# Delta-rule recurrence and MLP on one core: first chunk's inverse in 64x64 tiles, and a new hand-written order of all queues

## The chip, the cores and the metric

The kernel runs on one core of a Trainium2 chip. The core has a matrix engine (TensorE, PE in the profile; its weight loads are PEld), VectorE (DVE), ScalarE (ACT), GpSimd (POOL) and SyncE (SP), which here only issues DMAs. Each engine works off its own list of instructions in order. Matrix results go to PSUM, eight banks of 2 KB a partition, which GpSimd can't read. The metric is the time of one execution in microseconds on the device; lower is better.

## The reference

There are 4 x 8 = 32 heads with 768 steps and a head dimension of 48. Each head keeps a 48x48 state that is read by the query and corrected by the delta rule; the rows of all heads of a step, 384 numbers, then go through an MLP with 2048 hidden units.

```python
k_n = k / (np.linalg.norm(k, axis=-1, keepdims=True) + 1e-06)
for t in range(S):
    y[:, :, t] = np.einsum('bhd,bhde->bhe', q[:, :, t], state)
    v_old = np.einsum('bhde,bhd->bhe', state, kt)
    state = state + bt[:, :, :, None] * np.einsum('bhd,bhe->bhde', kt, vt - v_old)
...
x = y.transpose(0, 2, 1, 3).reshape(B * S, H * D)
out = gelu_tanh(x @ w_in) @ w_out
```

The line for the output stands before the update, so a step does not see its own key.

## The kernel before, in words

The 768 steps are cut into 12 chunks of C = 64. Within a chunk the recurrence is solved with matrices: with A the strictly triangular 64x64 matrix of scaled key products of a head, the corrected values are (I + A)^-1 (v - K S), and what a chunk adds to the state and to the output are plain products. The partitions hold two batches at once (64 steps each), so a **unit** u is 16 of the 32 heads and a chunk has two units, 2c and 2c+1; there are 24.

`prep(u)` (line 461) makes a unit ready. kn, kb and qb are the normed keys (L476), the keys times beta (L478) and the queries, in bf16. T transposes them on TensorE (L486) and kT copies them out; from unit 10 on a DMA does that. G2 and G (L508, L500) are the products of keys; ln and wp (L512, L516) copy them under a mask into tiles whose other triangle was written beforehand ("backgrounds", `tri` for ln and `triw` for wp, in `preset`, line 371). Then comes the inverse, five iterations in the loop from L521 on. Two 64x64 blocks stand on the diagonal of a 128x128 tile bd, so one matmul of 128 rows does both batches. X1 (L525, GpSimd) puts the first estimate there, one half at a time; A (L535) multiplies bd with wp or ln, rt (L542, VectorE) adds twice the identity, B multiplies bd with that, and the result goes back into bd in two half copies (bde, by ScalarE or VectorE), or once into the compact tile xi and from there by GpSimd (bdc, L529). The last result is xi. In the last two iterations only the columns from 16 or 32 on are made (A16, A32).

`chain(c)` (line 554) is what must go chunk by chunk: K and R (keys times state, less v), U (xi times that, L601), S (the state's update, L610), O and Q (output, L624, L579), X (its transposition, L645). For the first chunk K, Q and R are replaced by a copy of v. `mlp(gi)` (line 652) takes the 256 rows of a chunk: 16 groups `up` of three matmuls (L666), four GELUs, and two rows of four `down` groups of four matmuls (L678), whose results go out through SP.

**What sets the order.** Nothing is dynamic. `ORDER` holds a list for each engine, written out as text, and `BANKS` the PSUM bank of each TensorE operation that takes one. `Flow.schedule` gives each operation its place and `Flow.emit` puts a semaphore wait ahead of what needs one. An operation that may run on several engines names them, and the lists decide. A label is the operation's name and a running number. **Fills** (`warm_up`, line 392) are matmuls of 128x512 on zeros that no one reads; they stand in TensorE's list where the clock is to be kept up. 97 of them stand there, 87 ahead of U.0.

**Loads.** `load` reads q, k and v of a chunk in three rotating buffers (SP's list; the first chunk's k in halves, also by ScalarE). `weights` (line 427) has four transfers of 768 KB, which GpSimd issues; its list stands still meanwhile. They are declared as readers of the second and third chunk's k and q, so that they wait until those have come.

Of the kernel before, what the change touches and what calls it, by code (L numbers as in the profile page):

```python
# [5 lines left out]
F32 = mybir.dt.float32  # L6
BF16 = mybir.dt.bfloat16
# [11 lines left out]
        fill.0 fill.1 fill.2 fill.3 fill.4 fill.5 fill.6 fill.7 fill.8 fill.9 fill.10 fill.11 fill.12 fill.13 fill.14 fill.15 fill.16  # L19
        fill.17 fill.18 fill.19 fill.20 fill.21 fill.22 fill.23 fill.24 fill.25 fill.26 fill.27 betaT.0 fill.28 fill.29 fill.30  # L20
        fill.31 fill.32 fill.33 fill.34 fill.35 fill.36 fill.37 fill.38 T.0 fill.39 fill.40 T.1 G2.0 G.0 fill.41 fill.42 fill.43
        fill.44 fill.45 G2.1 G.1 fill.46 fill.47 fill.48 fill.49 fill.50 A.0 fill.51 fill.52 fill.53 fill.54 B.0 A.3 fill.55 fill.56
        fill.57 fill.58 B.5 A.1 fill.59 fill.60 fill.61 fill.62 fill.63 B.1 A.4 fill.64 fill.65 fill.66 fill.67 B.6 A.2 fill.68
        fill.69 fill.70 A.5 fill.71 fill.72 B.2 fill.73 B.7 T.2 fill.74 fill.75 fill.76 fill.77 A16.1 A16.0 fill.78 G2.2 fill.79 B.8
        B.3 fill.80 T.3 A32.1 fill.81 fill.82 A32.0 fill.83 B.9 B.4 G.2 fill.84 G2.3 fill.85 fill.86 U.0 fill.87 fill.88 A.6 G.3 S.0
        fill.89 B.10 O.0 K.0 fill.90 fill.91 fill.92 A.7 A.9 T.4 B.11 X.0 B.15 fill.93 fill.94 fill.95 fill.96 A.8 G.4 up.4 A.10 up.5
        B.12 up.6 B.16 up.8 A16.2 up.9 up.7 up.10 A.11 up.11 B.13 G2.4 up.0 B.17 up.1 up.12 up.2 up.13 up.3 up.14 A16.3 A32.2 A.12
        up.15 T.5 B.18 down.4 B.20 down.5 G2.5 G.5 A32.3 B.14 down.6 B.19 A.13 down.7 Q.0 U.1 B.21 down.0 A.15 O.1 A.14 B.25 down.1
        S.1 X.1 down.2 B.22 A.16 K.1 down.3 B.26 A16.4 up.20 up.28 up.21 up.29 B.23 A.17 T.6 up.30 B.27 up.31 up.22 G2.6 up.23 A16.5
        A32.4 G.6 up.24 B.28 up.16 up.25 up.17 A.18 up.18 A32.5 B.24 up.19 B.30 up.26 T.7 B.29 T.8 up.27 A.19 down.12 G2.7 G.7 G2.8  # L30
        B.31 down.13 G.8 U.2 down.14 A.20 down.15 A.21 A.24 B.32 T.9 B.35 down.8 A16.6 B.40 down.9 G2.9 Q.1 O.2 G.9 B.33 down.10 A.22
        X.2 A.25 down.11 B.36 A32.6 up.36 A.27 up.37 B.34 B.41 up.38 A.23 B.45 up.32 up.39 up.33 B.37 up.34 up.40 up.35 up.41 A.28
        up.42 A16.7 A.26 up.43 up.44 B.46 down.20 B.38 B.42 up.45 S.2 up.46 A32.7 down.21 A16.8 up.47 A.29 B.39 down.16 B.43 K.2
        down.22 B.47 down.23 Q.2 U.3 down.17 A32.8 A16.9 down.18 O.3 S.3 down.19 X.3 B.48 G2.10 G.10 B.44 up.52 up.60 up.53 K.3 G2.11
        up.61 up.54 up.62 A32.9 up.63 A.30 up.56 up.55 up.57 B.50 up.58 G.11 B.49 up.59 up.48 A.31 up.49 U.4 G2.13 A.33 B.51 up.50
        up.51 G.13 Q.3 O.4 G2.12 B.55 A.39 X.4 A.32 G.12 down.28 B.65 up.64 B.52 A.34 up.65 up.68 up.66 A.40 up.67 A.36 up.69 B.56
        A16.10 up.70 B.66 B.60 up.71 up.76 B.53 up.77 A.35 up.78 A.37 up.79 down.24 A.41 B.61 B.57 up.72 A32.10 down.25 A16.11 B.67
        A.38 down.26 up.73 B.58 S.4 B.62 up.74 A16.13 down.27 up.75 A16.12 down.29 K.4 B.68 B.54 A32.11 down.32 B.63 B.59 down.33
        down.36 U.5 Q.4 down.34 A32.12 down.35 O.5 A32.13 down.37 G2.14 S.5 G.14 down.38 B.64 B.69 down.39 K.5 G2.15 G.15 down.30 U.6
        Q.5 A.42 down.31 up.80 A.45 up.81 B.70 up.82 O.6 A.43 up.83 up.92 G2.17 G.17 up.93 up.84 up.94 B.71 B.75 up.95 up.85 G2.16  # L40
        up.86 A.46 up.87 G.16 up.88 B.76 up.89 A.51 up.90 A.44 A.48 up.91 B.85 A.47 B.72 down.40 B.80 up.104 down.41 B.77 up.105 A.52
        A.49 down.42 up.106 B.81 up.107 A16.14 down.43 up.100 B.86 up.101 A16.15 up.96 B.73 up.97 up.102 B.78 up.103 up.98 A.50 up.99
        A32.14 A.53 up.108 B.82 up.109 A32.15 S.6 up.110 B.79 B.87 up.111 down.44 K.6 B.74 A16.16 down.45 A16.17 U.7 B.83 B.88 down.46
        down.48 Q.6 S.7 down.49 O.7 G2.18 G.18 down.47 down.50 A32.17 A32.16 down.51 G2.19 K.7 A.54 B.84 down.52 B.89 B.90 down.53
        G.19 down.54 A.55 U.8 G2.20 G.20 down.55 A.57 up.120 B.91 up.121 B.95 up.122 G2.21 up.123 A.60 G.21 A.58 A.56 B.100 up.124
# [87 lines left out]
class Flow:  # L133
# [34 lines left out]
    def schedule(self, order, banks):  # L168
        seen, label = {}, {}
        for o in self.ops:  # L170
            kind = o.name.lstrip("01")
            label[f"{kind}.{seen.setdefault(kind, 0)}"] = o
            seen[kind] += 1
# [102 lines left out]
def bass_deltanet__then__act_gelu_tanh_kernel(  # L276
# [13 lines left out]
    NU = 2 * NC  # L290
    DIRECT = lambda u: (2, 3, 4, 5) if u < 8 else (2, 4)
    GROUPS = [[c] for c in range(NC)]
    TURN, TURNX = 10, 5

    F = Flow()
    A = F.add

    with nc.allow_non_contiguous_dma("strided loads"), nc.allow_low_precision("bf16 pipeline"):
# [39 lines left out]
        def hf(a, n=C):  # L338
            return slice(64 * a, 64 * a + n)
# [406 lines left out]
```

## Time and profile before

| what | value |
|---|---|
| median of 3 runs | 283.89 us (283.83 to 288.8) |
| the profiled execution | 283.22 us |
| its span, first to last instruction | 281.5 us |
| mean granted TensorE clock | 0.981 |
| DMA traffic | 29.71 MB, mean 106 GB/s |

The profile is of one execution. Its page gives the busy time of each engine, then the span in 40 slices of 7 us with a digit for each (tenths busy; PEclk is the clock that was granted to TensorE, in tenths), then the DMA queues, the chain of work that ended last, and the costliest groups of instructions. In a group or a timeline the row reads: line, engine, operation, tiles out<-in, shape, count, then busy time and idle time with the engine that ended it. "issue" means that the engine waited for nothing that the profile shows. Queue q0 carries the transfers that GpSimd asks for, q1 those of SP and ScalarE, and q8 and q14 are named "instruction". The windows view cuts the span in stretches and gives for each the length, then busy time and count of each engine, the granted clock, the mean share of the DMA engines' time (over 1 where packets queue) and the rate. The span outside the program (1.7 us of the execution's time) is the same for every kernel.

### The profile page before, as it was taken

Reading aid. Unit: us, or ns where it says so; the run is one execution under the profiler, and the core shown is the slowest. Engines: PE = TensorE matmul, PEld = TensorE weight load, DVE = VectorE, ACT = ScalarE, POOL = GpSimd, SP = SyncE. Lnnn points to the kernel's source line nnn. Section 1 sums busy time; section 2 is a strip of 40 time slices with the busy share of each in tenths; the row PEclk is TensorE's granted clock in tenths of the full one; section 3 lists DMA queues with packets and bytes.
Section 4 is the critical chain, followed back from the end, with each engine's and each line's share of the span. In section 5 each row is a group of like instructions: output and inputs, shape, how many; then the busy total and the mean of one; then the engine's idle time right before and its main releaser. Section 6 shows DMA issues by size and latency. Waiting matters only on the chain.

```text
span 281.5 us, 12649 instructions
## 1 busy us (share of the span) xinstructions
PE 264.2 (94%) x5726; PEld 200.4 (71%) x5737; DVE 198.9 (71%) x307; ACT 173.5 (62%) x261; POOL 144.9 (51%) x224
## 2 busy tenths in 40 slices
PE   8999957999999999979999899999999989999994
PEld 3555645877887887758876678976788777778762
DVE  6488963899899977867776699866898576752000
ACT  7678544788776976475872476645686546523541
POOL 3376653179895899767653872845546132110000
PEclk9999995999999999997999999999999999999999
DMA  5999999942919519996546980498819330043004
GB/s 106 164 153 180 189 191 149 153 75 41 133 36 175 105 33 174 143 152 135 94 88 121 160 123 2 87 171 144 156 30 148 68 72 2 2 56 73 21 14 98
DMA packets 109237, 29.71 MB, mean 106 GB/s; under 512 B 103296, under 2 KB 108416, under 8 KB 109184
## 3 DMA queue, kind: packets, MB, share of 16 engines
q1 hardware_dynamic: 105696, 25.57, 58.2%
q0 software_dynamic: 2880, 3.15, 7.2%
q8 instruction: 45, 0.74, 1.2%
q10 hardware_dynamic: 608, 0.20, 0.3%
q14 instruction: 8, 0.07, 0.1%
HBM read 20.64 MB, written 4.72 MB: 90 GB/s over the span
## 4 chain that ended last, share of the span: by engine, by line
PE 82%; DVE 6%; issue 4%; POOL 4%; ACT 2%; DVEq 0%; POOLq 0%
PE ps L666 22%; PE ps L678 21%; PE ps L535 19%; PE ps L394 6%; PE ps L579 2%; PE ps L486 2%; PE ps L624 2%; PE ps L508 2%; POOL nrm L455 2%; PE ps L601 2%; PE ps L500 2%; PE ps L610 1%; DVE wp L516 1%; DVE ln L512 1%; POOL tok L478 1%
## 5 line engine op out<-in xcount | busy, mean ns | idle before, releaser
L666 PE MATMUL ps<-xT,W 128*128 128x256 bf16 x576 | 83.0, 273 | 0.0
L678 PE MATMUL ps<-W,gT 128*128 128x384 bf16 x384 | 76.5, 328 | 0.7 <-issue 0.7
L342 ACT ACTIVATE bd<-ps 64x512 bf16<-64x512 f32 x93 | 54.2, 589 | 25.7 <-PE ps L535 24.0
L671 ACT ACTIVATE gT<-ps 128x1024 bf16<-128x1024 f32 x48 | 48.5, 1022 | 23.9 <-PE ps L666 23.6
L542 DVE TENSOR_TENSOR rt<-ps,two 128x512 bf16<-128x512 f32 x72 | 48.2, 687 | 11.7 <-PE ps L535 10.8
L666 PEld LDWEIGHTS ps<-xT,W 128*128 128x128 bf16 x576 | 48.7, 98 | 7.3 <-ACT gT L671 0.3
L525 POOL TENSOR_SCALAR_AFFINE_SELECT bd<-ln 64x512 bf16<-64x512 bf16 x48 | 31.4, 657 | 32.9 <-DVE ln L512 29.5
L529 POOL COPY bd<-xi 64x256 f32<-64x256 f32 x64 | 25.3, 397 | 39.7 <-ACT xi L342 24.9
L678 PEld LDWEIGHTS ps<-W,gT 128*128 128x128 bf16 x384 | 32.6, 98 | 17.2 <-issue 1.4
L342 ACT ACTIVATE xi<-ps 128x512 bf16<-128x512 f32 x42 | 24.4, 595 | 16.0 <-PE ps L535 15.8
L516 DVE CAST_PREDICATED wp<-mup,ps 128x1024 bf16<-128x1024 uint16 x24 | 29.0, 1214 | 2.3 <-PE ps L500 2.3
L542 DVE TENSOR_TENSOR rl<-ps,two 128x384 bf16<-128x384 f32 (+1 forms) x48 | 22.8, 485 | 9.2 <-PE ps L535 8.8
L535 PE MATMUL ps<-rt,bd 128*128 128x64 bf16 x576 | 28.7, 195 | 0.3 <-issue 0.2
L455 POOL TENSOR_TENSOR nrm<-nrm,half 128x16 f32<-128x16 f32 x9 | 26.4, 2928 | 4.2 <-DVE nrm L452 4.0
L535 PEld LDWEIGHTS ps<-rt,bd 128*128 128x128 bf16 x576 | 24.3, 99 | 5.5 <-DVE rt L542 2.4
L535 PE MATMUL ps<-wp,bd 128*128 128x64 bf16 (+1 forms) x576 | 27.3, 189 | 0.5 <-DVE rt L542 0.2
L478 POOL TENSOR_TENSOR tok<-tok,bsb 128x384 bf16<-128x384 bf16 x24 | 20.2, 850 | 14.6 <-DVE tok L476 7.7
L535 PEld LDWEIGHTS ps<-wp,bd 128*128 128x128 bf16 x576 | 23.6, 98 | 5.5 <-issue 1.5
L342 DVE CAST bd<-ps 64x512 bf16<-64x512 f32 x35 | 24.0, 686 | 4.9 <-PE ps L535 4.4
L394 PE MATMUL ps<-wz 128*128 128x512 bf16 x86 | 24.5, 410 | 2.2 <-DVE wz L348 1.3
L476 POOL TENSOR_TENSOR tok<-kraw,nrm 128x384 bf16<-128x384 f32 x22 | 18.1, 829 | 6.8 <-DVE nrm L459 6.7
L342 ACT ACTIVATE ob<-ps 128x384 f32<-128x384 f32 x20 | 9.7, 490 | 18.9 <-PE ps L678 18.6
(84 smaller groups left out, 341.9 us busy)
## 6 DMA issues: line engine op xcount, KB each, us to landing
qraw<-in_q_dram SPq DMA_DIRECT2D x24, 192.0 KB, 5.5
vraw<-in_v_dram SPq DMA_DIRECT2D x24, 192.0 KB, 5.5
out_dram<-ob SPq DMA_DIRECT2D x47, 96.0 KB, 3.1
kraw<-in_k_dram SPq DMA_DIRECT2D x22, 192.0 KB, 4.8
W<-in_moe_w_in_dram POOLq DMA_DIRECT2D x2, 768.0 KB, 8.6
W<-in_moe_w_out_dram POOLq DMA_DIRECT2D x2, 768.0 KB, 10.3
kraw<-in_k_dram SPq DMA_DIRECT2D x3, 96.0 KB, 3.4
kT<-tok SPq DMA_TRANSPOSE x14, 4.6
```

The costliest lines, as they stand in the source:

```text
L342: return e.activation(out, in_, ACT.Copy) if e is nc.scalar else e.tensor_copy(out, in_)
L394: return e.matmul(P(f"fill{i}")[:, :], wz[:, 0:128], wz[:, 0:512])
L455: e.tensor_tensor(nr[:, 1, hx], nr[:, 0, hx], half[:, hx], ALU.pow),
L478: A(POOL, z + "kb", lambda e, P: e.tensor_tensor(kb, kn, bcol, ALU.mult), reads=[n("tok0"), *BS], writes=[n("tok1")], pos=u)
L516: A("dve", z + "wp", lambda e, P: e.copy_predicated(wp[s][:, :, :], mup[:, :].bitcast(U16).unsqueeze(1).to_broadcast([128, H, 2 * C]), P(p ...
L525: A("pool", z + "X1", lambda e, P, src=src, dst=dst: e.affine_select(out=dst, in_=src, compare_op=ALU.not_equal, fill=1.0, base=0, pattern ...
L529: A("pool", z + "bdc", lambda e, P, src=src, dst=dst: e.tensor_copy(dst.bitcast(F32), src.bitcast(F32)), reads=[n("xi")], writes=[w(f"bd{a ...
L535: ins = e.matmul(P(name)[:, C * h + lo:C * h + C], bd[m][:, h, :], rhs[:, h, lo:C])
L542: A("dve", z + f"rt{lo or str()}", lambda e, P, i=i, lo=lo, r_=r_: e.tensor_tensor(r_[:, :, lo:C], P(ps(f"A{i}")).rearrange("p (h t) -> p ...
L666: ins = e.matmul(P(ph)[:, w * f:w * f + w].rearrange("p (x t) -> p x t", x=2), W1[:, j, 128 * (i + f):128 * (i + f) + 128], x_[:, :, j, :] ...
L671: A("act", z + "gelu", lambda e, P, i=i, ph=ph: e.activation(g_[:, i:i + nf, 0:w], P(ph).rearrange("p (f t) -> p f t", f=nf), ACT.Gelu_app ...
L678: ins = e.matmul(P(po)[:, 0:DM], g_[:, f, 128 * b:128 * b + 128], W2[:, f, :], start=(f == 0), stop=(f == FC - 1))
```

## The change

Six things are changed at once.

1. For units 0 and 1 (`TILED` = 2) the inverse runs in the compact tile xi. X1t is one addition of ln and twice the identity on GpSimd or VectorE, without bd. Each product At or Bt is 16 matmuls of 64x64, two tiles of the array, in place of 8 of 128x128. The result is copied once into xi. All 64 output rows are made as before, and the last two At start at columns 16 and 32.
2. For these two units the masked copy wp is cut in two (wph), so that the inverse waits for the first half alone, and O for the second ("wq").
3. GpSimd may write the backgrounds; the new lists let it write triw for three of the six wp tiles and tri for one of the four ln tiles. For units 2 to 5 VectorE may scale the keys (the lists leave that on GpSimd) and ScalarE may copy the queries (it does so for units 2 and 3). kT of any unit may be copied by ScalarE (unit 9 is).
4. The weight transfers no longer wait for other loads. In GpSimd's list two of them now stand side by side behind unit 3's kb, the third behind X1 of unit 2, the last behind kn of unit 5.
5. Labels are name.position/number instead of name.number.
6. All five lists and the banks are new. There are 111 fills. 87 stand ahead of the first U, 99 ahead of the first up, and the others singly or in threes up to chunk 8.

```diff
-    TURN, TURNX = 10, 5
+    TURN, TURNX, TILED = 10, 5, 2
...
-                    A(("act", "dve"), z + ("tri" if w == C else "triw"), lambda e, P, t=t, w=w: copy(
-                        e, t[s][:, :, :], tmpl[:, 0:w].unsqueeze(1).to_broadcast([128, H, w])), reads=["tmpl", "tmplz"], writes=[f"{n}{s}"], pos=2 * s - 9)
+                    A(("act", "dve", "pool"), z + ("tri" if w == C else "triw"), lambda e, P, t=t, w=w: copy(
+                        e, t[s][:, :, :], tmpl[:, 0:w].unsqueeze(1).to_broadcast([128, H, w])) if e is not nc.gpsimd else
+                      e.tensor_copy(t[s][:, :, :].bitcast(F32), tmpl[:, 0:w].bitcast(F32).unsqueeze(1).to_broadcast([128, H, w // 2])),
+                      reads=["tmpl", "tmplz"], writes=[f"{n}{s}"] + ([f"wq{s}"] if w > C else []), pos=2 * s - 9)
...
-                  reads=[f"{n}raw1{x}" for n in "kq" for x in range(2)], writes=[f"W1{i}"], dma=f"w1{i}", pos=-3 + 0.1 * i)
+                  writes=[f"W1{i}"], dma=f"w1{i}", pos=-3 + 0.1 * i)
...
-                  reads=[f"{n}raw2{x}" for n in "kq" for x in range(2)], writes=[f"W2{i}"], dma=f"w2{i}", pos=-2 + 0.1 * i)
+                  writes=[f"W2{i}"], dma=f"w2{i}", pos=-2 + 0.1 * i)
...
+            if u < TILED:
+                A(("dve", "pool"), z + "X1t", lambda e, P: e.tensor_tensor(
+                    xi[s][:, :, :], ln[m][:, :, :], two[:, :].unsqueeze(1).to_broadcast([128, H, C]), ALU.add), reads=[w("ln"), "two"],
+                  writes=[n("xi")], pos=u)
+                for i in range(1, 6):
+                    con, conn = (wp[s][:, :, 0:C], n("wp")) if i % 2 else (ln[m], w("ln"))
+
+                    def product(e, P, name, rhs, lo):
+                        for h in range(H):
+                            for a in range(2):
+                                ins = e.matmul(P(name)[hf(a), C * h + lo:C * h + C], xi[s][hf(a), h, :], rhs[hf(a), h, lo:C])
+                        return ins
...
+                    A(EV, z + "xi", lambda e, P, i=i: copy(e, xi[s][:, :, :].rearrange("p h t -> p (h t)"), P(ps(f"B{i}"))),
+                      frees=[ps(f"B{i}")], writes=[n("xi")], pos=u)
+                return
```

The start of the new lists of TensorE (from the first T to the first up) and of GpSimd:

```diff
+        fill/31 fill/32 fill/33 fill/34 fill/35 fill/36 fill/37 fill/38 fill/39 fill/40 fill/41 T.0/0 fill/42 fill/43 fill/44 fill/45
+        fill/46 fill/47 fill/48 T.1/0 G2.0/0 G.0/0 fill/49 fill/50 fill/51 fill/52 fill/53 G2.1/0 fill/54 fill/55 At.0/0 G.1/0 fill/56
+        fill/57 fill/58 Bt.0/0 fill/59 At.1/0 fill/60 At.0/1 fill/61 fill/62 Bt.1/0 fill/63 fill/64 fill/65 fill/66 At.1/1 Bt.0/1
+        fill/67 fill/68 fill/69 Bt.1/1 At.0/2 fill/70 fill/71 T.2/0 Bt.0/2 At.1/2 fill/72 fill/73 At.0/3 Bt.1/2 fill/74 T.3/0 At.1/3
+        Bt.0/3 G2.2/0 fill/75 fill/76 Bt.1/3 fill/77 fill/78 fill/79 fill/80 fill/81 At.1/4 At.0/4 G.2/0 fill/82 Bt.1/4 Bt.0/4 fill/83
+        fill/84 fill/85 fill/86 A.2/0 U.0.5/0 G2.3/0 fill/87 fill/88 B.2/0 fill/89 O.0.7/0 G.3/0 S.0.5/0 fill/90 fill/91 fill/92
+        fill/93 fill/94 A.2/1 X.0.8/0 fill/95 fill/96 fill/97 A.3/0 B.2/1 K.2.5/0 fill/98 up.3.25/0 B.3/0 up.3.25/1 A.2/2 T.4/0
...
+        tmplz.-11/0 masks.-12/2 bdz.5/0 two.-12/0 two.-12/1 ident.-29/0 triw.-9/0 masks.-12/0 triw.-7/0 ident2.-29/0 half.-28/0
+        bdz.4/0 kb.0/0 bdz.2/0 mup.-12/0 kb.1/0 mup.-12/1 masks.-12/1 mlo.-12/0 mlo.-12/1 X1t.0/0 X1t.1/0 kn.2/0 kb.2/0 kn.3/0 kb.3/0
+        tri.-3/0 w1.-3/0 w2.-1.9/0 kn.4/0 X1.2/1 triw.-1/0 X1.2/0 w1.-2.9/0 pow.6/0 X1.3/1 X1.3/0 eps.6/0 qb.5.01/0 kb.4/0 qb.4.01/0
+        kn.5/0 w2.-2/0 sq.8/0 kn.7/0 kn.6/0 X1.4/0 X1.4/1 bdz.3/0 kb.5/0 X1.5/1 X1.5/0 pow.8/0 qb.7.01/0 eps.8/0 kb.6/0 kn.9/0 kn.8/0
```

A label such as T.0/0 is the transposition of unit 0; in the text it is written T.0, and chain operations by their chunk (U.0 for U.0.5/0).

235 lines of the change are left out of this document (135 added, 100 removed), and 18 rows, old and new, of the table BANKS.

## The prediction

> **What bounds the kernel now.** I read the page first: the busy times, the slices, the shares of the chain.
>
> ```profile
> PE 264.2 (94%) x5726; PEld 200.4 (71%) x5737; DVE 198.9 (71%) x307; ACT 173.5 (62%) x261; POOL 144.9 (51%) x224
> ...
> PEclk9999995999999999997999999999999999999999
> DMA  5999999942919519996546980498819330043004
> ...
> PE 82%; DVE 6%; issue 4%; POOL 4%; ACT 2%; DVEq 0%; POOLq 0%
> ```
>
> TensorE is the bound from end to end, but two things on these lines are not arithmetic: 4% of the chain is "issue", time in which TensorE waited for nothing the profile shows, and the slices hold one dip of the clock to half and one to 0.7. The chain of waits, cut to 34 to 52 us, shows the largest piece, and the prices that I use for single operations.
>
> ```profile
> 34.47 0.61 PE ps L601 x32
> ...
> 36.20 0.56 issue
> ...
> 37.01 0.32 PE ps L610 x32
> ...
> 40.18 3.58 issue
> ...
> 50.15 0.23 PE ps L535 x8
> 50.38 0.33 PE ps L666 x3
> ```
>
> TensorE stops for 3.58 us in the middle of one transpose group, whose data were ready. To see why, I cut the windows view at the two stops above and at later ones, and at equal counts of instructions between them.
>
> ```profile
> core 0: us, PE busy (x) PEld busy (x) DVE busy (x) ACT busy (x) POOL busy (x), PEclk, DMA share, GB/s
> 14.66:22.62 7.96, 7.65 (x141) 4.31 (x140) 6.58 (x11) 6.55 (x10) 4.52 (x7) 1.00 1.33 150
> 22.62:30.86 8.24, 7.77 (x131) 5.00 (x131) 7.46 (x13) 6.09 (x12) 5.45 (x8) 1.00 1.24 186
> 30.86:36.76 5.90, 4.87 (x129) 3.42 (x129) 5.10 (x9) 3.20 (x7) 5.17 (x8) 1.00 1.32 191
> 36.76:43.76 7.00, 3.10 (x125) 2.47 (x127) 3.47 (x4) 2.69 (x4) 3.61 (x6) 0.88 1.32 192
> 43.76:52.96 9.20, 8.98 (x124) 7.28 (x125) 5.91 (x9) 5.62 (x9) 1.73 (x3) 0.72 0.92 145
> 59.65:63.30 3.65, 3.65 (x139) 2.81 (x140) 3.52 (x7) 3.00 (x5) 2.04 (x5) 1.00 0.11 20
> 121.17:126.57 5.40, 3.30 (x139) 2.66 (x133) 3.38 (x5) 3.91 (x6) 3.23 (x5) 1.00 1.10 146
> 223.08:226.54 3.46, 2.70 (x149) 2.10 (x141) 2.52 (x4) 0.81 (x1) 1.94 (x4) 1.00 0.12 26
> ```
>
> From one stop to the next, 36.76 to 43.76, stand 127 weight loads and as many matmuls (two matmul records are missing): 256 instructions with two that wait for semaphores. The other windows are cut at the same count (those full of small matmuls also count the ones that reach over an edge), and the stops fall on such edges. The DMA view says what TensorE waits for; the first line is from 35.2 to 40.6 us, the second from 40.6 to 42.2.
>
> ```profile
> q0 software_dynamic: 963, 0.73, 99.2%
> ```
>
> ```profile
> q8 instruction: 1, 0.02, 5.9%
> ```
>
> The queue of instructions moved nothing up to 40.6, while q0, which carries only the MLP weights that GpSimd asked for, took nearly the whole of the engines; then one block of 16 KB came and TensorE went on at 43.76. So TensorE runs on blocks of 256 instructions, the next but one is asked for when a block ends, and a block can't pass faster than its successor arrives. The rows give that time where TensorE was starved: 5.90 and 7.00 us with weights under way, 5.40 with loads alone (121.17), 3.46 in quiet (DMA share 0.12). At 59.65 a block passed in 3.65 us without a stop. The Trainium skill, "Runtime: NRT & Kernel Launch", section "Instruction fetch mechanics", has the blocks of 256 but says that crossing a boundary is "mostly hidden"; the 3.58 us row speaks against it here, and what its rule would make of the time is the second rival.
>
> **The change part by part.**
>
> Compact products. Each of 20 products (two units, five A and five B) becomes 16 matmuls of 64x64 in place of 8 of 128x128. An old one takes 0.23 us (the x8 row). For a new one the nearest row is U, the same shape of diagonal tiles with 48 columns: 0.61 us for 32, so 0.31 for 16, and 0.41 if it grows with 64 columns. I take 0.36, both ends kept: 20 x 0.13 = 2.6 us more TensorE time (1.6 to 3.6), and 320 instructions more. The Trainium skill, "TensorEngine Tiling (Array Packing)", section "Key Properties", says that different tiles can execute in parallel; by it 16 halves would take what 8 wholes took, and the 2.6 would be 0. The U row, whose tiles are in the same two quadrants, does not show that gain whole.
>
> What it gives back is evacuation. An iteration of the first units ran like this:
>
> ```profile
> 16.68 1.25 PE L394 MATMUL ps<-wz 128*128 128x512 bf16 x5
> 17.77 0.40 PE L535 MATMUL ps<-wp,bd 128*128 128x64 bf16 x8
> ```
>
> ```profile
> 19.57 1.21 ACT L342 ACTIVATE bd<-ps 64x512 bf16<-64x512 f32 x2 [0.87 <-PE ps L535]
> ```
>
> ```profile
> L342 ACT ACTIVATE xi<-ps 128x512 bf16<-128x512 f32 x42 | 24.4, 595 | 16.0 <-PE ps L535 15.8
> ...
> L478 POOL TENSOR_TENSOR tok<-tok,bsb 128x384 bf16<-128x384 bf16 x24 | 20.2, 850 | 14.6 <-DVE tok L476 7.7
> ```
>
> Two half copies (1.21 us) become one whole (0.595): 0.6 us saved an iteration, less 2 x 0.13 for the slower products, so 0.35 x 5 = 1.7 us on the chain. X1 on GpSimd becomes an addition of 512 columns, 850 x 512/384 = 1.1 us against two selects. Splitting wp in two costs VectorE some 0.3 us. But the fills decide when the chain may go: the new order puts 42 fills and the beta transposes ahead of T.0 and 7 more ahead of T.1. At 0.217 us a fill (five from 16.68 to 17.77),
>
> ```profile
> 1.25 7.81 PE L394 MATMUL ps<-wz 128*128 128x512 bf16 x28 [1.25 <-DVE wz L348]
> 8.99 0.93 PE L406 MATMUL ps<-identf,braw 32*128 32x32 f32 x12
> ...
> 14.54 0.32 PE L508 MATMUL ps<-kT 48*64 48x64 bf16 x16
> ```
>
> the 28 ahead of betaT become 26, which starts at 8.6; 16 more fills put T.0 at 12.9, 7 more T.1 at 15.1, and G2.0 comes at 15.8 to 16.0 against 14.54. The chain starts 1.4 us later and gains 1.7: U.0 stays at about 34.5. ScalarE issues two more loads ahead of its table load, and the first half of k goes first on SP; both are covered by the fills that hold T.0 until 12.9, and would cost about one issue (0.8 us) without them.
>
> GpSimd writes two wp backgrounds before it scales keys, and one more and one of ln behind; it waited then and has room (51% busy). The keys of units 2 to 5 stay on GpSimd, so that freedom is not used. Cost 0, covered by those waits; uncovered it is 0.75 us a background.
>
> Fills. Both orders have 87 ahead of the first U; behind it 10 become 24. That is 14 x 0.217 = 3.0 us of TensorE time, free only where TensorE would have waited.
>
> Weights. Four transfers of 768 KB were asked for at these times:
>
> ```profile
> 18.89 1.01 POOL L432 DMA_DIRECT2D W<-in_moe_w_in_dram  x1
> 23.76 0.83 POOL L476 TENSOR_TENSOR tok<-kraw,nrm 128x384 bf16<-128x384 f32 x1 [3.86 <-DVE nrm L459]
> ...
> 26.24 0.82 POOL L432 DMA_DIRECT2D W<-in_moe_w_in_dram  x1
> ...
> 31.85 0.94 POOL L436 DMA_DIRECT2D W<-in_moe_w_out_dram  x1
> ...
> 38.10 0.94 POOL L436 DMA_DIRECT2D W<-in_moe_w_out_dram  x1
> ```
>
> The dropped reads do not bring them forward: in GpSimd's new order they stand behind kn.2 (which waits for the second chunk's norm, in the old order at 23.76), kb.2, kn.3, kb.3 and a background, so the first two go at 28 and 29, next to each other, the third behind X1.2 near 34, the fourth behind kn.5 near 41. Behind each issue, 1 us, stand X1.2 and kn.4, which have that slack. By the page's list of DMA issues the slower pair lands like this,
>
> ```profile
> W<-in_moe_w_out_dram POOLq DMA_DIRECT2D x2, 768.0 KB, 10.3
> ```
>
> which is in time for the first up and down. What it does cost is that weights are under way from 28 to 52, when the new order's blocks are shortest.
>
> The sum. I counted matmuls in the new PE order, two instructions each and one more in a hundred for semaphores, the first edge at the same count as before, and priced them by the rows (up 0.33, A and B 0.23, K, Q and S 0.32, U and O up to 0.6, and from the next two the down group; the second is chunk 1's U in the timeline of TensorE).
>
> ```profile
> 58.10 0.65 PE ps L678 x4
> ```
>
> ```profile
> 62.62 0.67 PE L601 MATMUL ps<-rs,xi 64*64 64x48 bf16 x32
> ```
>
> The edges fall in G2.0 (16.0 us), At.0/1, At.1/2, behind fill 79, at U.0, X.0, G.4, T.5 and at the end of chunk 1's U. The blocks between them last 4.8, 5.4, 4.7, 4.1, 4.0, 4.8, 7.3 and 4.8 us. The old first blocks lasted 7.96 and 8.24 and hid their fetches. With 5.1 us for the first (engine waits), 5.4 for the second, 6.45 (mean of 5.90 and 7.00) for each of the next four, which can't hide it, and 7.3 and 4.8: 16.0 + 5.1 + 5.4 + 25.8 + 7.3 + 4.8 = 64.4. In the old trace that U ended at 63.2 (62.62 and 0.6). So the start is 1.2 us later. By the same prices TensorE has 197.7 us of work behind that point in the old order and 200.3 in the new: 2.6 more. Together +3.8 us. The order of the rest is new throughout, and no row prices that: from below it is the loss of every later stop (the first rival), from above as many again; I take 0, since the counts of later blocks with under 3.6 us of work are alike (seven now, eight before). The profiled execution took 283.22 us (span 281.5); the median of the runs stands 0.67 above it. 283.2 + 3.8 + 0.7 = 287.7, say 287.5.
>
> **The rivals.** Faster: fetches do not starve the start. Then U.1 ends at its price, 55.8, plus the waits of the old start (U.0 came at 34.5 with 31.7 us of work ahead of it, so 2.7), at 58.5, or 4.7 us before the old one; less the 2.6, with the 7 fills behind U.1 in waits (1.5) and one later stop and the half-clock window behind it gone,
>
> ```profile
> 126.58 0.32 PE L508 MATMUL ps<-kT 48*64 48x64 bf16 x15 [1.84 <-issue]
> ```
>
> ```profile
> 45.40:48.80 3.40, 3.18 (x36) 2.19 (x38) 1.98 (x4) 3.15 (x5) 0.09 (x1) 0.50 0.83 140
> 127.40:130.80 3.40, 3.40 (x46) 2.47 (x43) 2.66 (x4) 1.86 (x3) 2.93 (x4) 0.50 0.42 83
> ```
>
> 1.84 and half of 3.4, it comes to -4.7 + 2.6 - 1.5 - 3.5 = -7.1: 276.8 us. For it: the new blocks are evener, none under 4 us in the first 50. Against it: 4 us is still below 5.9. The rule of the Trainium skill's "Runtime: NRT & Kernel Launch" on fetches, named above, would end here.
>
> Slower: the two weight transfers asked for side by side hold a fetch longer than one did. If that adds 1.5 us to the measured 7.00 in two of the four blocks, it is 2 x (8.5 - 6.45) = 4.1 on top of the forecast: 291.8 us. It decides over 2% once the four blocks average 6.93 us, and 7.00 is a measured row. A stop of 3 us also halves the clock, as the row from 45.40 shows; that is in the old time as well, so it isn't added.
>
> No change: the waits absorb the products and the fills, and the weights' fetches stop TensorE as long as now: 284.
>
> **How the numbers follow.** The forecast (287.5; its own range is 284 to 290, by the ends 5.90 and 7.00 in four blocks, 2.2 each way, and of the products, 1.0) gets 0.33, the starved start 0.34, the free start 0.25, no change 0.08. Two per cent, about what a measurement of this kernel can tell from no change, is 278.2 and 289.6. Faster: 0.22 of the free start's 0.25. Slower: 0.34 and 0.02 of the forecast's. The rest, 0.42, is within. The range 277 to 293 leaves out some 0.12 of the free start below and 0.08 above.
>
> **What would show it.** Right: the "issue" pieces between 25 and 50 us sum to over 5 us and lie on edges of 256 instructions, the first up comes at 46 us or later, U.0 at 34 or later. A compact product of 0.31 to 0.41 us confirms the 2.6; 0.23 does not. It is wrong if the clock stays at 1.0 through 50 us and the first up comes at 42, or if a block there passes in under 4.5 us with weights under way.

## The result, and the profile after

The changed kernel takes 280.98 us (279.01 to 283.71, eight runs), the kernel before beside it 284.29 (283.74 to 288.8). The ratio is 0.9871, with a 95% interval of 0.9829 to 0.9914: 1.3% faster, clear of no change but under two per cent, where 287.5 us, 1.3% slower, was forecast. The ratios, and the medians from the next section on, are of those executions that lie within 1.5% of the fastest of their kernel; ranges are of all. The profiled execution took 279.01 us, its span is 277.2, the mean granted clock 0.998.

The page of the changed kernel, the same lines as of before:

```profile
PE 263.3 (95%) x5895; PEld 200.0 (72%) x5911; DVE 197.6 (71%) x306; ACT 168.3 (61%) x252; POOL 147.2 (53%) x226
...
PEclk9999999999999999999999999999999999999999
DMA  7996999990494679973489880659658121224004
...
PE 91%; DVE 5%; issue 2%; ACT 0%; DVEq 0%
```

"issue" fell from 4% of the chain to 2%, and both dips of the clock are gone. TensorE is busy for as long as before, though it now runs at full clock throughout: it has more to do. The chain of waits in the stretch that the prediction is about:

```profile
36.15 0.61 PE ps L665 x32
36.76 0.04 PE ps L545
36.80 0.67 issue
37.47 0.32 PE ps L545 x15
...
41.63 0.43 PE ps L431 x2
42.06 1.67 issue
43.73 0.38 PE ps L431
...
45.17 0.49 PE ps L730 x3
```

U.0 (36.15) comes 1.7 us later than before, the first up (45.17) 3.9 us earlier. The stops are 0.67 and 1.67 us instead of one of 3.58; the second stands between two fills, which lie at 41.63 and 43.73. The windows view, cut at the edges of 256 instructions:

```profile
core 0: us, PE busy (x) PEld busy (x) DVE busy (x) ACT busy (x) POOL busy (x), PEclk, DMA share, GB/s
16.77:22.08 5.31, 5.00 (x133) 2.81 (x136) 4.91 (x8) 3.23 (x6) 2.32 (x2) 1.00 1.32 142
22.08:27.66 5.58, 5.26 (x136) 3.45 (x134) 4.92 (x11) 3.40 (x7) 3.38 (x5) 1.00 0.57 103
27.66:32.35 4.69, 4.37 (x139) 3.21 (x135) 4.43 (x11) 3.58 (x9) 2.80 (x4) 1.00 0.89 138
32.35:37.47 5.12, 4.20 (x129) 2.91 (x129) 4.51 (x7) 4.92 (x8) 3.85 (x6) 1.00 1.16 190
37.47:43.73 6.26, 4.28 (x126) 3.02 (x128) 4.22 (x6) 2.36 (x4) 5.82 (x8) 1.00 1.21 203
43.73:48.32 4.59, 4.36 (x123) 4.02 (x126) 3.48 (x5) 2.64 (x5) 4.21 (x5) 1.00 0.87 129
48.32:56.10 7.78, 7.67 (x146) 6.23 (x140) 7.34 (x12) 6.01 (x10) 3.09 (x4) 1.00 1.08 174
56.10:61.10 5.00, 5.00 (x130) 3.72 (x129) 4.22 (x6) 3.62 (x7) 1.62 (x3) 1.00 1.23 155
```

The blocks that were to be held at 6.45 us each are the third to the sixth. They lasted 4.69, 5.12, 6.26 and 4.59. U.1 ends at 61.1, before at 63.2, forecast 64.4.

For the whole span I summed the pieces of over 0.1 us in which TensorE was idle at an edge of 256 ("stops" from here on; a wait that ends within eight instructions of an edge counts): 8.7 us before, 3.7 after, so 5.0 less. The half clock inside the run (42.1 to 48.9 and 127.4 to 130.8 before, none after) is the other part. TensorE was busy for 8.3 of these 10.2 us, 3.18 and 3.40 of them in the two rows at half clock that the prediction shows; taking half of that as lost (an estimate) gives 4.2. That makes 9.2 us; the span fell by 4.3. Some 5 us were given back as more work and longer chains; the first experiment shows them again.

### The profile page after: what moved, and what is told of

Read it like the earlier page. It is cut to its first block, busy times and chain, and to the rows that moved or that the text cites. A ratio compares the mean times of both kernels' runs of the same rounds, so it can differ in the third digit from the quotient of the medians.

```text
span 277.2 us, 12977 instructions
## 1 busy us (share of the span) xinstructions
PE 263.3 (95%) x5895; PEld 200.0 (72%) x5911; DVE 197.6 (71%) x306; ACT 168.3 (61%) x252; POOL 147.2 (53%) x226
## 4 chain that ended last, share of the span: by engine, by line
PE 91%; DVE 5%; issue 2%; ACT 0%; DVEq 0%
PE ps L742 23%; PE ps L730 23%; PE ps L599 19%; PE ps L431 9%; PE ps L643 2%; PE ps L688 2%; PE ps L665 2%; PE ps L537 2%; PE ps L523 2%; PE ps L570 2%; PE ps L545 2%; DVE wp L555 1%; PE ps L674 1%; DVE rt L606 1%; DVE kT L377 1%
## 5 line engine op out<-in xcount | busy, mean ns | idle before, releaser
L735 ACT ACTIVATE gT<-ps 128x1024 bf16<-128x1024 f32 x48 | 48.7, 1021 | 25.8 <-PE ps L730 25.7
L377 ACT ACTIVATE bd<-ps 64x512 bf16<-64x512 f32 x83 | 48.8, 589 | 14.4 <-PE ps L599 13.2
L606 DVE TENSOR_TENSOR rt<-ps,two 128x512 bf16<-128x512 f32 x66 | 44.1, 684 | 14.3 <-PE ps L599 13.8
L589 POOL TENSOR_SCALAR_AFFINE_SELECT bd<-ln 64x512 bf16<-64x512 bf16 x44 | 28.8, 656 | 28.2 <-DVE ln L549 25.1
L377 ACT ACTIVATE xi<-ps 128x512 bf16<-128x512 f32 x46 | 27.2, 595 | 24.1 <-PE ps L599 18.7
L431 PE MATMUL ps<-wz 128*128 128x512 bf16 x95 | 27.5, 411 | 4.4 <-issue 2.9
L555 DVE CAST_PREDICATED wp<-mup,ps 128x1024 bf16<-128x1024 uint16 (+1 forms) x26 | 29.4, 1135 | 2.2 <-PE ps L537 2.0
L599 PE MATMUL ps<-rt,bd 128*128 128x64 bf16 x528 | 25.8, 193 | 0.6 <-DVE wp L555 0.5
L599 PE MATMUL ps<-wp,bd 128*128 128x64 bf16 (+1 forms) x528 | 24.5, 187 | 0.6 <-DVE wp L555 0.6
L377 DVE CAST bd<-ps 64x512 bf16<-64x512 f32 x29 | 20.0, 688 | 3.4 <-PE ps L599 2.6
L549 DVE CAST_PREDICATED ln<-mlo,ps 128x512 bf16<-128x512 uint16 x24 | 16.3, 684 | 6.5 <-PE ps L545 6.4
```

What stands on the lines that cost most here:

```text
L377: return e.activation(out, in_, ACT.Copy) if e is nc.scalar else e.tensor_copy(out, in_)
L431: return e.matmul(P(f"fill{i}")[:, :], wz[:, 0:128], wz[:, 0:512])
L555: A("dve", z + ("wp" if nh == 2 else "wph"), lambda e, P, cs=cs, nh=nh: e.copy_predicated(wp[s][:, :, cs], mup[:, cs].bitcast(U16).unsquee ...
L589: A("pool", z + "X1", lambda e, P, src=src, dst=dst: e.affine_select(out=dst, in_=src, compare_op=ALU.not_equal, fill=1.0, base=0, pattern ...
L599: ins = e.matmul(P(name)[:, C * h + lo:C * h + C], bd[m][:, h, :], rhs[:, h, lo:C])
L606: A("dve", z + f"rt{lo or str()}", lambda e, P, i=i, lo=lo, r_=r_: e.tensor_tensor(r_[:, :, lo:C], P(ps(f"A{i}")).rearrange("p (h t) -> p ...
```

## Experiments

The theory: the time that the change moved lies in the stops and in the clock that follows them, and both depend on which instructions the edges of 256 fall on, which any edit ahead of them moves. The rival: the change gains by what it does, by lighter evacuation and a better order.

### The edges moved, and nothing else

The first fills are made of four matmuls of 128 columns. That is six instructions more a fill, ahead of everything else. The first transposition, at 12.65 us in the kernel before and at 13.77 in the changed one, starts between 12.8 and 14.2 in these versions, in no order of the number of fills cut.

```diff
+        SPLIT = [0, 1, 2, ... 20]
...
             def fill(e, P, i):
+                if i in SPLIT:
+                    for y in range(4):
+                        ins = e.matmul(P(f"fill{i}")[:, 128 * y:128 * y + 128], wz[:, 0:128], wz[:, 0:128])
+                    return ins
                 return e.matmul(P(f"fill{i}")[:, :], wz[:, 0:128], wz[:, 0:512])
```

With 21 fills the edges move by 126 instructions (`half_block`); with 11, 27, 32 and 37 by 66, 162, 192 and 222.

after_half_block: 

> The changed kernel with 21 of its first 26 fills made of four matmuls of 128 columns instead of one of 512: same time on TensorE, 126 instructions more, so every edge of a block of 256 instructions behind them falls half a block elsewhere in the same order. Fetch theory (the gain is that TensorE stops less for its instructions, because this order's edges and short blocks fall well): the stops on edges rise from 3.3 us in sum to 6 or more, and the time from 281 to 283 or more. Rival (the gain is lighter evacuation and fewer waits for other engines): 281 within 0.6, since nothing but the edges moved. If edges fall by chance in both orders: the time moves by 1 to 2 us either way.

before_half_block: 

> The kernel before with the same 21 fills split, so its edges move by half a block too. Fetch theory: the stops of 3.58, 1.84, 0.82, 0.70 and 0.76 us leave their places, and the time moves by more than 1 us, more likely down (they stood badly), to 279 to 283. Rival: 284.3 within 0.6.

after_quarter_block: 

> The changed kernel with its first 11 fills made of four matmuls of 128 columns: 66 instructions more, so that every edge of 256 lies a quarter of a block earlier in the work. If the place of the edges sets the stops (theory), the stops between 25 and 50 us move to other groups, the idle time at edges leaves 4.6 us by over 1.5 either way, and the total follows it; over the four places of the edges the changed kernel and the one before have means within 1.5 us of each other. If the change itself brings its gain (rival: fewer engine waits from the compact form and the new order), this stays at 280 to 282 us.

before_quarter_block: 

> The kernel before with the same 66 instructions more. Theory: the 3.58 us stop at 40.2 moves or goes, the total is anywhere between 277 and 288 and follows the idle time at edges. Rival (the change itself gains): 284 within 1 us, and 3 us above the changed kernel with the same edges.

after_threequarter_block: 

> The changed kernel with its first 32 fills made of four matmuls of 128 columns: 192 instructions more, edges three quarters of a block earlier. Theory: as with a quarter of a block, a new set of stops, and a total between 278 and 288 that follows the idle time at edges. Rival: 280 to 282.

before_threequarter_block: 

> The kernel before with 192 instructions more. Theory: a total between 277 and 288 that follows the idle time at edges, and a mean of the four places within 1.5 us of the changed kernel's. Rival: 284 within 1 us.

before_fiveeighths_block: 

> The kernel before with its first 27 fills made of four matmuls of 128 columns: 162 instructions more. Theory: a total between 277 and 285 that follows the idle time at edges; with 66, 126 and 192 more this kernel took 281.6, 282.4 and 279.9, so the old place of the edges was worse than its neighbours. Rival (place of the edges does not matter, the chip's spread does): 284 within 1 us.

before_seveneighths_block: 

> The kernel before with its first 37 fills made of four matmuls of 128 columns: 222 instructions more, close to a whole block, where the edges come back to 34 instructions from their old places. Theory: between 279 and 285, its stop in the first T of chunk 1 back in part. Rival: 284 within 1 us.

after_fiveeighths_block: 

> The changed kernel with its first 27 fills made of four matmuls of 128 columns: 162 instructions more. If the change by itself costs and its gain was the place of the edges (theory), this takes 282 or more, at least 4 us more than the kernel before with the same edges (276.7). If the change by itself gains (rival) and 162 is simply a good place, this takes 274 or less.

after_seveneighths_block: 

> The changed kernel with its first 37 fills made of four matmuls of 128 columns: 222 instructions more. Theory: 283 to 288, above the kernel before with the same edges (281.5), idle time at edges of 6 us or more. Rival: 278 or less.

Moved by a whole block of 256 (fill 0 in nine pieces, fills 1 to 40 in four), the edges fall on the old instructions again:

before_whole_block: 

> The kernel before with 256 instructions more in its first 41 fills: one whole block, so the edges behind them fall on the same instructions as in the kernel before. If the place of the edges sets the time (theory), it comes back to 283 to 286, with a stop of 2.5 us or more in the first T of chunk 1, although it has more instructions ahead than the versions that took 277 to 282. If the smaller fills themselves made those faster (rival), this takes 280 or less.

In the table, the median is of the runs; all else is of the one profiled execution. "Rest" is its time less the stops and less half of what TensorE was busy at half clock (the estimate from above).

| kernel, moved by | median | profiled | stops | busy at half clock | rest |
|---|---|---|---|---|---|
| before, 0 | 284.0 | 283.2 | 8.7 | 8.3 | 270.4 |
| before, 66 | 281.6 | 281.7 | 8.4 | 6.8 | 269.9 |
| before, 126 | 277.5 | 277.5 | 6.6 | 0 | 270.9 |
| before, 162 | 276.7 | 278.1 | 5.6 | 3.2 | 270.9 |
| before, 192 | 279.1 | 277.0 | 5.0 | 6.2 | 269.0 |
| before, 222 | 280.8 | 283.0 | 7.9 | 10.2 | 270.0 |
| before, 256 | 284.5 | 286.1 | 10.5 | 9.1 | 271.0 |
| after, 0 | 281.0 | 279.0 | 3.7 | 0 | 275.3 |
| after, 66 | 283.4 | 283.3 | 7.2 | 3.2 | 274.5 |
| after, 126 | 285.5 | 286.6 | 8.3 | 6.1 | 275.3 |
| after, 162 | 292.2 | 289.8 | 10.8 | 8.7 | 274.7 |
| after, 192 | 289.7 | 288.5 | 10.8 | 3.4 | 276.0 |
| after, 222 | 285.9 | not used | | | |

(The 277.5 is the least certain median: the ten executions of that version lie between 276.3 and 284.4. One of the four executions with 222 in the changed kernel took 641.18 us, and it is the profiled one; more on it at the end.)

The rest hardly moves: 269.0 to 271.0 in the seven profiles of the kernel before, 274.5 to 276.0 in the five of the changed one. So the stops and the half clock carry the whole spread between places, and with both taken out the change costs 4.9 us (275.15 less 270.29 in the mean).

The chain of before_whole_block shows that it is the place:

```profile
41.62 0.06 PE ps L490
41.68 3.58 issue
45.26 1.33 PE ps L490 x11
```

The stop is back at 3.58 us, in the same transpose group of chunk 1, one matmul in, as in the kernel before; with fewer instructions added the longest stop there lay in other groups and took 1.9 to 3.5 us, and the time moved with it. In the changed kernel an added half block puts the stop into the compact products (the chain of after_half_block; L576 are the products there):

```profile
34.69 0.41 PE ps L576 x14
35.09 2.07 issue
37.16 0.47 PE ps L576 x18
...
42.79 0.95 issue
```

So the gain of 3 us is smaller than what moving the edges does to either kernel: 276.7 to 284.5 before, 281.0 to 292.2 after. The place that the change happened to have is the best of its six; the old one, and its repetition a block later, are the worst of the old kernel's. That it came out faster is luck of the place. The rivals' times (284 within 1 us before, 280 to 282 or less after) were missed at every place to which the edges were moved, and so was the expectation that both kernels have the same mean over the places (within 1.5 us): over the six common places the means are 280.0 and 286.3. The differences, after less before, are -3.1, 1.8, 8.0, 15.5, 10.6 and 5.1: 6.3 on average with a standard error of 2.7, which alone would leave it open whether the change costs; the rest settles it. The theory's own ranges were wide, and three were missed: 277.5 and 276.7 before (126 and 162) lie below theirs, 289.7 after (192) above.

### The compact form undone

`TILED` is 0, with the changed order: A and B on bd, two half copies an iteration, X1 by GpSimd as two selects. 23 fills made of eight matmuls of 64 columns give back 322 instructions for the 320 that go.

```diff
-    TURN, TURNX, TILED = 10, 5, 2
+    TURN, TURNX, TILED = 10, 5, 0
...
-        ... At.0/0 G.1/0 fill/56 fill/57 fill/58 Bt.0/0 fill/59 At.1/0 fill/60 At.0/1 ...
+        ... A.0/0 G.1/0 fill/56 fill/57 fill/58 B.0/0 fill/59 A.1/0 fill/60 A.0/1 ...
```

after_untiled_filled: 

> The changed kernel with the first two units in the old form: block-diagonal tiles, two half copies an iteration, products of 8 matmuls of 128x128; 23 fills made of eight matmuls of 64 columns give back the 322 instructions that this saves, so that the later edges stay in their places. If the gain comes from where the edges fall (theory), this stays within 2 us of 281 where the later edges keep their places, with the first U at 36 to 38. If it comes from the lighter evacuation of the compact form (rival), the first U comes 1.7 us or more later, at 37.8 or later, and the total is 284 or more with no more idle time at edges.

285.31 us (283.07 to 287.03). The first U in its chain of waits, and ahead of it one of the half copies that it waited for:

```profile
34.98 0.59 ACT bd L377
...
39.17 0.62 PE ps L671 x28
```

The rival was right on this part, in the first U and in the total, and the theory's 2 us were missed. U.0 comes 3.1 us later (39.17 against 36.08; from G2.0 on 3.7, as G2.0 itself was 0.6 earlier), U.1 and U.2 1.6 us later (62.08 and 84.84 against 60.47 and 83.23). The other 2.7 us of the total come at 124.7, in a stop of 1.77 us with half clock behind it, which the changed kernel has not:

```profile
123.50:126.90 3.40, 1.20 (x69) 0.93 (x67) 0.76 (x2) 1.69 (x2) 3.26 (x6) 1.00 0.11 14
126.90:130.30 3.40, 3.40 (x83) 2.89 (x76) 3.18 (x4) 1.71 (x3) 1.42 (x5) 0.50 0.71 146
```

So the compact form is worth 1.6 us at the second chunk in this order; the remainder of the 4.3 is again a fetch. With the stops taken out as in the table above (4.1 us, and 3.4 busy at half clock) the rest is 278.0, 2.7 above the changed kernel's: by this count the form is worth 2.7.

### The late fills

after_thin_fills, the changed kernel:

```diff
+                n = 16 if i >= 87 else 512
-                return e.matmul(P(f"fill{i}")[:, :], wz[:, 0:128], wz[:, 0:512])
+                return e.matmul(P(f"fill{i}")[:, 0:n], wz[:, 0:128], wz[:, 0:n])
```

> The changed kernel with its 24 fills behind the first U of 16 columns instead of 512: the same count of instructions, so the edges lie in the same places, and 24 x 0.2 = 4.8 us less of TensorE work. If those fills lie on TensorE's path (theory: 3.0 us of the change's own cost), the time falls by 3 to 5 us, to 276 to 278; if they only fill waits (rival 1), it stays within 1 us of 281; if the blocks that lose them end before their next one has come (rival 2, fetch), stops between 37 and 50 us grow by what the fills lost, and the clock dips to half there.

283.0 us (280.41 to 288.23), 2 us slower with 4.8 us less of work, so the theory and rival 1 both failed. The difference is small: beside the kernel before the ratio is 0.9928 (0.9893 to 0.9962), and its interval overlaps that of the change itself (up to 0.9914) a little; what is clear is that no time was saved. The stops in this stretch hardly grew (1.20 and 1.51 us), so rival 2 failed in its size; but the clock fell to half for 10.2 us (windows of after_thin_fills), and for 3.4 more behind a stop of 1.00 us at 124.9:

```profile
35.50:38.90 3.40, 2.16 (x107) 1.81 (x105) 2.00 (x5) 1.97 (x3) 2.99 (x2) 1.00 1.27 186
38.90:42.30 3.40, 2.16 (x53) 1.98 (x54) 2.89 (x5) 1.20 (x2) 3.10 (x6) 0.51 1.18 212
```

In the changed kernel, TensorE was busier in these windows and the clock held:

```profile
33.60:37.00 3.40, 2.95 (x105) 2.20 (x99) 3.34 (x5) 3.22 (x7) 2.41 (x4) 1.00 1.18 191
37.00:40.40 3.40, 2.61 (x107) 2.10 (x110) 2.34 (x4) 1.64 (x3) 3.11 (x3) 1.00 1.28 187
```

Then more late fills in the kernel before, with its edges: those from 87 on made of two or three matmuls of 512 columns (14 more), 228 instructions more ahead.

before_whole_late_fills: 

> The kernel before with the ten fills behind its first U made of 24 matmuls of 512 columns, and 228 instructions more in its first 38 fills: the edges from the end of the late fills on are those of the kernel before. If late fills cost what they last (forecast), it takes 3.0 us more than the run with 256 more. If they hold the clock (theory since the thin fills), the half clock between 42 and 49 us goes or halves, and it takes 1 to 3 us less.

283.98 us (282.54 to 286.29), 0.6 less than with the 256 alone; the intervals of the two ratios overlap (0.9992 to 1.0074 and 1.0022 to 1.0116). The half clock went (10.2 us to none), as the theory had it, and the stop of 3.58 became 2.19; but the rest rose from 271.0 to 274.5, by the 3.0 us of work and a little more, which took nearly all of it back. Neither forecast size was right: they pay for themselves and no more.

### The weights

All four transfers are asked for one after the other, behind X1 of unit 2 in the kernel before (with the reads dropped there as well), behind the second X1t in the changed one.

```diff
-        ... X1t.0/0 X1t.1/0 kn.2/0 ...
+        ... X1t.0/0 X1t.1/0 w1.-3/0 w1.-2.9/0 w2.-2/0 w2.-1.9/0 kn.2/0 ...
```

before_weights_early: 

> The kernel before with its four weight transfers asked for one behind the other right after the first X1 (about 19 to 23 us), their reads of other loads dropped, and nothing else changed; they should be under way from 19 to about 38 us instead of 19 to 48. Fetch theory, with weights as what holds the fetch: the stop of 3.58 us at 40 us goes or falls under 1 us, the clock stays at full speed through 50 us, and the time falls by 4 to 6 us to 278 to 280. If ordinary loads hold it as well: the stop stays over 2 us and the time within 1.5 us of 284.3. Rival: the loads of q, k and v come later behind the weights, and the time rises by 1 to 3 us.

after_weights_early: 

> The changed kernel with its four weight transfers asked for one behind the other right after the two X1t (about 21 to 25 us). Fetch theory: the stops of 0.67 us at 36.8 and 1.67 us at 42.1 go, since no weights are under way at 37 to 42, and the time falls by 1.5 to 2.5 us to about 279. Rival: no gain (281), or up to 2 us slower because the loads that the second chunk needs come later.

284.7 and 285.2 us: no gain in the kernel before, and 4.2 us lost in the changed one, more than its rival allowed. In the kernel before, no stop at an edge of over 0.5 us is left ahead of 90 us, but TensorE stood still for 6.50 us from 42.35 on, and the chain ran through a load (before_weights_early):

```profile
21.41 22.60 DMA qraw<-in_q_dram
```

which took 22.60 us beside the weights. In the changed one it was a load of k, 15.67 us, and stops of 1.21 and 1.30 us came at 27.7 and 33.9. The two profiled executions took 290.8 and 290.6 us, over 5 us more than the medians; so that asking earlier moves the trouble from the fetches to the loads is what they suggest, not shown for the medians.

### The fastest version

The kernel before with its edges moved by 162, and 14 or 5 more late fills, the early pieces fewer by as many instructions:

before_fiveeighths_late: 

> The kernel before with 134 instructions more in its first 23 fills and the ten fills behind its first U made of 24 matmuls of 512 columns: behind the late fills its edges are those of the version that took 276.7 us. If late fills gain by the clock they hold (3.4 us at half, so 1.7) and lie in waits else, 274 to 276; if their 3.0 us lies on the path and the clock only pays half of it back, 277 to 279.

before_fiveeighths_half_late: 

> The same with five more late fills instead of 14, and 152 instructions more in its first 28 fills. If the late fills around the stop at 38 us are what holds the clock, this gets the 1.7 us with 1.1 us of work: 275 to 277. If the place of the edges by itself sets the time, 276 to 278, with one window of half clock as before.

With 14: 280.3 us (277.84 to 281.86), 3.6 slower than without and above both of its forecasts. With 5: 275.5 (273.4 to 278.23; ratio to before 0.9677, 0.9562 to 0.9791), not to be told from without (276.72; ratio 0.9729, 0.9673 to 0.9785); the half clock went, as the first reading had it. The versions with 5 and with none both beat the changed kernel. The page of the one with 5:

```profile
PE 262.7 (96%) x5818; PEld 202.5 (74%) x5818; DVE 198.3 (72%) x307; ACT 173.7 (63%) x261; POOL 144.5 (53%) x224
...
PEclk9999999999999999999999999999999999999999
...
PE 84%; DVE 6%; POOL 4%; issue 2%; ACT 2%; DVEq 0%; POOLq 0%
```

No dip of the clock, and 4.4 us of stops in the whole span. It is the old kernel, old products and order, with some fills cut in pieces and five doubled. Taking the best of several places favours chance, but the place of 162 was built twice, with and without the five, and was fast both times.

## Why the prediction was wrong, by its steps

**The bound.** That TensorE stops at edges of 256 instructions while a fetch is under way held, and so did the places: the third block ends behind fill 79 (at 32.56; its window is cut one fill early, at 32.35), the fourth in G2.3 next to U.0, the fifth behind X.0, the sixth in G.4, the seventh in T.5. The mechanism is shown by before_whole_block, and by a count that I made over all traces but that of the 641 us execution: of 93 stops of over 0.5 us at an edge, 92 ended 1.2 to 1.8 us after a block of instructions had landed on q8 (median 1.45; the stop of 3.58 us: 1.57). In the changed kernel's trace exactly one such block lands between every two edges. The Trainium skill, "Runtime: NRT & Kernel Launch", section "Instruction fetch mechanics", calls the crossing "mostly hidden". Most edges do pass without a stop; but where they lay moved the time by 11 us in the changed kernel, so here the rest is not small.

**"6.45 (mean of 5.90 and 7.00) for each of the next four, which can't hide it".** This step failed, in the words "each of": 25.8 us, measured 20.7. Two of the four were held, the fourth (5.12 us, with the stop of 0.67) and the fifth (6.26, with 1.67). The other two got their fetches through before or between the weights, as the DMA view of the changed kernel shows for the first 1.5 us of the third block and the first 1.3 us of the sixth:

```profile
q1 hardware_dynamic: 990, 0.19, 65.1%
q8 instruction: 1, 0.02, 4.5%
```

```profile
q0 software_dynamic: 72, 0.12, 50.4%
q8 instruction: 1, 0.02, 5.8%
```

The third block begins at 27.66, 0.2 us before the first weights are asked for at 27.90: no q0 yet, and its fetch landed at 29.11. The sixth begins at 43.73, 2 us before the third transfer had landed, and the fourth is asked for at 43.91: q0 at half, and its fetch landed at 46.20. While the fourth block ran, from 32.4 on, q0 had it all:

```profile
q0 software_dynamic: 259, 0.52, 101.4%
q1 hardware_dynamic: 134, 0.03, 8.3%
```

The price itself was not far off. From a block's first instruction to the landing of the next fetch, over the same traces, it took 4.7 us in the median where q0 had over 0.3 of the DMA engines in the 3 us that follow (63 fetches), 2.7 where q1 had over half and q0 nothing (453; nine in ten under 3.8), and 1.8 in quiet, with q0 at nothing and q1 under a fifth (230; under 2.5). With the 1.45 until TensorE goes on, that is 6.2, 4.2 and 3.3 us for a block that is held. I had the price for a fetch behind the weights and put it on four blocks, without laying the weights' own times (28, 29, 34 and 41, in the same text) beside the edges. U.1 ended 3.3 us ahead of its forecast by this, with 0.8 lost ahead of the first edge (16.77 for 16.0) and some 1.1 in the other blocks.

**"The order of the rest is new throughout, and no row prices that".** This is the second step that failed: I took 0 beside 2.6 us of work. From U.1's end to the end of TensorE's work it was 214.3 us before (277.5 less 63.2) and 212.2 after (273.3 less 61.1): 2.1 less where 2.6 more was forecast. That is 4.7 us, more than the start gave. The old kernel stops there for 0.42, 1.84, 0.82, 0.70 and 0.76 us, the new one for over 0.3 us at one place alone,

```profile
203.61 1.00 issue
```

and the half clock from 127.4 is gone (1.7 us). That is some 5 us, so the work was sized about right. The loss of every later stop was in the text as the bound from below, and was nearly what came. It could as well have gone the other way: with 162 instructions more, the changed kernel's chain has

```profile
111.58 2.14 issue
```

and stops of 1.33 us at 130.2 and 1.27 at 154.1.

**Compact products, +2.6.** Too much. The timeline of TensorE in the changed kernel gives them by their starts:

```profile
25.52 0.44 PE L570 MATMUL ps<-rt,xi 64*64 64x64 bf16 x16
25.80 0.42 PE L570 MATMUL ps<-wp,xi 64*64 64x64 bf16 x16
...
27.35 0.44 PE L570 MATMUL ps<-rt,xi 64*64 64x64 bf16 x16
27.62 0.42 PE L570 MATMUL ps<-wp,xi 64*64 64x64 bf16 x16
```

0.27 to 0.28 us against 0.23, below the lower end of 0.31: 20 x 0.045 = 0.9 us. U, the row that I went by, has the same shape but is dearer for one matmul; what makes it so I did not try. The Trainium skill's "TensorEngine Tiling (Array Packing)", section "Key Properties", by which different tiles can execute in parallel, so that the halves would add nothing, was nearer than my row: the measured cost is 0.9 and not 0.

**Evacuation, -1.7, and U.0 "at about 34.5".** The direction is right: without the compact form U.0 is 3.1 us later and U.1 1.6. But against the old kernel the chain from G2.0 to U.0 shrank by 0.5 us (19.9 to 19.4) and not by 1.7. In both kernels TensorE waited for other engines for 0.5 us or less in that stretch, so a shorter copy had little wait to take away. U.0 came at 36.08, 1.6 later than forecast; 0.8 of it stood ahead of the chain, as G2.0 came at 16.71 and not at 15.8 to 16.0. These 0.8 may be spread: in after_thin_fills, with the same early list, G2.0 came at 15.97. X1t took 1.16 us (1.1 forecast).

**Fills, +3.0.** Right as a cost, wrong as the whole effect. They are work: 14 more in the kernel before raised the rest by 3.5 us at one place of the edges and by 2.6 at the other (273.5 against 270.9). But they also hold the clock: without their length the changed kernel is no faster, and by its median 2 us slower. In the kernel before, 14 more changed nothing that can be told at one place and cost 3.6 at the other. That "it is in the old time as well, so it isn't added" was said of the half clock in the old kernel; the point missed is that the new one could lose it. Over all traces, the windows of 3.4 us after which the clock fell from full to half had TensorE busy for 0.08 to 0.63 of their length, and no window over 0.63 was followed by a fall. The Trainium skill, "TensorE: Matmul & The Clock Gate", section "Part 1: The HAM clock gate (the "warmup" mystery)", has the clock go down after an idle window of some 3.4 us; the length agrees, but here 0.6 busy was not always enough to hold it, and one of 1.74 us in 3.40 (40.4 to 43.8 after the change) did hold it, so the limit isn't sharp.

**Weights.** Asked for at 27.90, 28.92, 34.66 and 43.91, forecast 28, 29, 34 and 41. That two side by side would hold a fetch past 7 us (the slower rival) did not happen in this kernel: the longest block is 6.26 in these four.

**The rivals.** "Fetches do not starve the start" set two marks: the clock stays at 1.0 through 50 us (it did), and a first up at 42 or a block under 4.5 us (45.17 and 4.59: neither). What came is half of it: U.1 ended at 61.1, between its 58.5 and my 64.4. Of the marks for the forecast, U.0 behind 34 came; the stops between 25 and 50 us sum to 2.3 and not to over 5, and the first up came ahead of 46. No rival said what the table says: that the place of the edges is a draw with a spread of some 8 us in the old kernel and 11 in the new, larger than the 3.8 us that my sum came to.

**What stays open.** Why single fetches take long in a given place: the medians go with the traffic, but which packets a request meets was not tried. And where the 4.9 us that the change costs with the stops taken out come from: the later fills account for some 3 of them and the compact form for 2.7 the other way, so that some 4.6 lie elsewhere in the new lists, which no run takes apart.

## What to carry to other kernels

Where a core is bound by small instructions, an edit that adds or removes some of them ahead of a busy stretch also moves the edges of its instruction blocks; compare two versions over several places (some fills cut in pieces are enough) before the difference is put down to the edit, and take the best place as a tuning step of its own, which here gave 7 us where the whole change gave 3. Lay the times of the large transfers beside the edges, block by block, before a fetch is priced. Filling matmuls are work wherever they stand; they pay only where they keep TensorE busy through a stretch after which its clock would fall.

## What was unexpected of the hardware

The 1.45 us between the landing of a block of instructions and TensorE's next one: a fetch that lands while TensorE waits costs that much again.

One execution of the changed kernel with 222 instructions more took 641.18 us. Its page:

```profile
PE 627.9 (98%) x6006; PEld 404.6 (63%) x6022; DVE 202.7 (32%) x306; ACT 171.6 (27%) x252; POOL 147.2 (23%) x226
```

TensorE's matmuls took 2.3 times as long, the other engines as long as ever, and the granted clock in the records is 1.000. Whatever slowed TensorE does not show in that row; the other three executions took 285.79 to 287.04 us.
